# Low parts of fp32 operands subtracted on GpSimd instead of VectorE, in the first two blocks of a gated scan and MLP kernel

## The chip, the core and the metric

The kernel runs on one core of a Trainium2 chip. A core has engines with queues of their own: TensorE (PE: matrix products into PSUM), VectorE (DVE), ScalarE (ACT), GpSimd (POOL) and SyncE (SP), whose queue issues the transfers here. Each engine takes its instructions in the order in which the program gives them, and semaphores make it wait for others. The metric is the device time of one execution in microseconds (us), as a median of several runs. It takes in a little more than the span of the profile, which goes from the first to the last instruction.

## What is computed

A linear attention with a complex gate for each key channel, and on its output an MLP with a piecewise activation:

```
a_n = a * min(|a|, 0.999) / (|a| + 1e-6)          # a complex, (B=4, H=8, S=768, D=48)
for t in range(S):
    S_re, S_im = (ar*S_re - ai*S_im) + outer(k[t], v[t]),  ar*S_im + ai*S_re
    y[t] = q[t] @ S_re
x = y as (3072 tokens, 384)
h = x @ w_in                                       # 384 -> 2048
g = where(h >= 1, h, where(h <= -1, 0, (h + 1)**2 / 4))
out = g @ w_out                                    # 2048 -> 384
```

All data are fp32. The two large products are made from rounded parts: each operand is split into a high part in the format fp32r and a low part, the operand less its high part, and a product is the sum of three matmuls: high by high, low by high and high by low. The change touches how low parts are made.

## The kernel before

**Units and blocks.** The 3072 tokens are 12 units of 256. Two units are a block, so there are six blocks (0 to 5) of T = 512 tokens. For a unit, `gates` makes the decay and the phase of the keys and queries (ScalarE and VectorE), `attend` the scores, masked products and states (TensorE, with `am` and `st` on VectorE), and the result lands transposed in the tile `xr`. For a block, `split` makes xH and xL of `xr`, and `moe` runs the MLP: for each of 16 slices f of the 2048 channels, `gemm1(f)` makes h in PSUM (three matmuls for each of three j; line 1160), the engines make g and its parts gh and gl, and `gemm2(f)` adds their products with the slice of w_out to three sums o in PSUM (line 1235).

**The activation.** In blocks 0 and 1 (`spare`, that is blk < SPARE = 2) ScalarE makes s from h in three instructions (lines 1185, 1195, 1199) and VectorE g = max(h, s) (line 1204). In the other blocks ScalarE has one instruction and VectorE two (1204 and 1212). Then ScalarE copies g to gh in fp32r (1218), and VectorE subtracts: gl = g - gh (1222). h lies in PSUM in two buffers, so gemm1(f + 2) needs g of slice f made; s and g share three buffers, and gh and gl share six.

**The weights.** Sixteen tiles of 128 x 768 (eight of w_in, wi; eight of w_out, wo; each serves two slices f) are loaded once as pairs of 32-bit words and decoded into fp32 by three VectorE instructions in place (`weights`, lines 431, 440, 449). ScalarE copies the high part (455). The low part of the first three tiles (n < LO_PE = 3) is made on TensorE through PSUM; of the 13 others VectorE subtracts it (460). From the fifth tile on, two staging buffers take turns, so the load of a tile waits for the subtraction of the tile two before it.

**The order.** Nothing is issued in the order in which the functions are written. Each `pl.op` notes an instruction for a planner: engine, a price in ns, what it reads and writes. `Plan.order` runs the whole program through a model of the five engines, with the prices and fixed delays between engines (LAT, 200 ns behind POOL); an engine takes of its ready instructions the one that is due first, where due times are worked back from those of the matmuls. The instructions are emitted in the order of the planned starts, so a price that changes can move any instruction of any engine, and what the model does not hold cannot move one. Before the first matmul of block 0, the planner also fills planned gaps of TensorE with small matmuls whose result is not used (line 1290), in numbers that follow from the planned times.

Of the kernel before, what the change touches and what calls it, by code (L numbers as in the profile page):

```python
# [10 lines left out]
F32 = mybir.dt.float32  # L11
# [4 lines left out]
ALU = mybir.AluOpType  # L16
# [274 lines left out]
def dve(n, two=False):  # L291
    return 66 + n / (1.92 if two else 0.96)


def act(n, ptr=False, acc=False, psum=False):
    return (80 if psum else 100) + (92 if ptr else 0) + (92 if acc else 0) + n * (0.77 if psum else 0.84)


def pe32(n):
    return 2 * max(85, n / 1.2 + 5)  # L300


def per(n):
    return n / 2.4 + 16
# [17 lines left out]
def gated_scan_moe(  # L322
    ctx: ExitStack, tc: tile.TileContext, kq, ari, art, v, wl, qn, kn, arn, ain, vn, out
):
    nc = tc.nc
# [38 lines left out]
    def tl(slot, shape, dtype, name, space=None):  # L364
        return pl.tile(
            slot, lambda: (space or sb).tile(shape, dtype, tag=slot, name=name, bufs=1)
        )
# [12 lines left out]
    def turn_of(tag, n):  # L380
        k = seen.get(tag, 0)
        seen[tag] = k + 1
        return f"{tag}{k % n}"

    V_, A_, PE_ = nc.vector, nc.scalar, nc.tensor
# [20 lines left out]
    def load(k, raw, eng="SP"):  # L406
        queue = nc.sync if eng == "SP" else nc.gpsimd
        queue.dma_start(raw.rearrange("p n t -> p (n t)"), wl[k].bitcast(U32))

    def weights(n, kind, i, slot):  # L410
        k = i + (NF // 2 if kind == "o" else 0)
        RAW = tl(slot, [P, 2 * DM, 2], U32, f"raw_{kind}{i}")
        Y = tl("y", [P, 2 * DM], U32, f"y_{kind}{i}")
        W = weight[kind, i] = tl(f"w{kind}{i}", [P, 2, 2, DM], F32R, f"w{kind}_{i}")
        hi, lo = (lambda: W.get()[:, :, 0]), (lambda: W.get()[:, :, 1])
        wide = lambda t: t.rearrange("p (e n) -> p e n", e=2)
        top, low = (lambda: RAW.get()[:, :, 1]), (lambda: RAW.get()[:, :, 0])
        N = 2 * DM
        eng, late = ("SP", 0) if n < 3 else (LOADS, LATE)
        pl.op(  # L420
            eng,
            SOFT_ISSUE if eng == "POOL" else DMA_ISSUE,
            lambda: load(k, RAW.get(), eng),
            w=[RAW],
            dma=P * N * 8 / LOAD,
            late=late,
        )
        pl.op(
            "DVE",
            dve(N, True),  # L430
            lambda: V_.tensor_scalar(
                Y.get(), top(), 3, 0x3FFFFFFF, op0=ALU.logical_shift_left, op1=ALU.bitwise_and
            ),
            r=[RAW],
            w=[Y],
        )
        pl.op(
            "DVE",
            dve(N),
            lambda: V_.scalar_tensor_tensor(  # L440
                low(), low(), 29, Y.get(), op0=ALU.logical_shift_right, op1=ALU.bitwise_or
            ),
            r=[Y],
            w=[(RAW, 0)],
        )
        pl.op(
            "DVE",
            dve(N),
            lambda: V_.scalar_tensor_tensor(
                low(), top(), 0xC0000000, low(), op0=ALU.bitwise_and, op1=ALU.bitwise_or  # L450
            ),
            w=[(RAW, 0)],
        )
        yf = lambda: wide(low().bitcast(F32))
        pl.op("ACT", act(N) + 50, lambda: A_.copy(hi(), yf()), r=[(RAW, 0)], w=[(W, 0)])
        if n >= LO_PE:
            pl.op(
                "DVE",
                dve(N),
                lambda: V_.tensor_tensor(lo(), yf(), hi().bitcast(F32), op=ALU.subtract),  # L460
                r=[(RAW, 0), (W, 0)],
                w=[(W, 1)],
            )
            return
        for e in range(2):
            R = tl("h0", [P, DM], F32, f"rest_{kind}{i}_{e}", ps)

            def rest(e=e, R=R):
                PE_.matmul(R.get(), ident, yf()[:, e], start=True, stop=False)
                PE_.matmul(R.get(), minus, hi()[:, e], start=False, stop=True)  # L470

            i_ = pl.op(
                "PE",
                pe32(DM) + per(DM),
                rest,
                r=[(RAW, 0), (W, 0)],
                w=[R],
                due=FIRST - 30000 + 2000 * n,
            )
            kinds[i_] = "rest"  # L480
            pl.op(
                "ACT",
                act(DM, psum=True),
                lambda e=e, R=R: A_.copy(lo()[:, e], R.get()),
                r=[R],
                w=[(W, 1 + e)],
            )
# [657 lines left out]
    def moe(blk):  # L1145
        XH, XL = split(blk)
        T = len(BLOCKS[blk]) * U
# [5 lines left out]
        def gemm1(f):  # L1153
            H = tl(turn_of("h", 2), [P, T], F32, f"h_{blk}_{f}", ps)
            for j in range(NJ):

                def mms(j=j):
                    sl = slice(j * P, (j + 1) * P)
                    for n, (part, x) in enumerate(((0, XH), (1, XH), (0, XL))):
                        PE_.matmul(  # L1160
                            H.get(),
                            weight["i", f // 2].get()[:, f % 2, part, sl],
                            x.get()[:, j, :],
                            start=j == 0 and n == 0,
                            stop=j == NJ - 1 and n == 2,
                        )

                kinds[len(pl.ops)] = "moe"
                pl.op(
                    "PE",  # L1170
                    3 * per(T),
                    mms,
                    r=[weight["i", f // 2]] + [(x, (ub, j)) for x in (XH, XL) for ub in range(len(BLOCKS[blk]))],
                    w=[H],
                    due=t0 + STEP * (f + j / 6),
                )
            SS = tl(turn_of("s", 3), [P, T], F32, f"s_{blk}_{f}")
            G = tl(turn_of("s", 3), [P, T], F32, f"g_{blk}_{f}")
            GH = tl(turn_of("gg", 6), [P, T], F32R, f"gh_{blk}_{f}")
            GL = tl(turn_of("gg", 6), [P, T], F32R, f"gl_{blk}_{f}")  # L1180
            spare = blk < SPARE
            pl.op(
                "ACT",
                act(T, ptr=True, psum=True),
                lambda: A_.activation(  # L1185
                    SS.get(), H.get(), AF.Relu, bias=c_half, scale=-0.5 if spare else 0.5
                ),
                r=[H],
                w=[SS],
            )  # L1190
            if spare:
                pl.op(
                    "ACT",
                    act(T, ptr=True),
                    lambda: A_.activation(SS.get(), SS.get(), AF.Relu, bias=c_one, scale=-1.0),
                    w=[SS],
                )
                pl.op(
                    "ACT", act(T), lambda: A_.activation(SS.get(), SS.get(), AF.Square), w=[SS]
                )  # L1200
            pl.op(
                "DVE",
                dve(T),
                lambda: V_.tensor_tensor(G.get(), H.get(), SS.get(), op=ALU.max),  # L1204
                r=[H, SS],
                w=[G],
            )
            if not spare:
                pl.op(
                    "DVE",  # L1210
                    dve(T),
                    lambda: V_.scalar_tensor_tensor(  # L1212
                        G.get(), SS.get(), 1.0, G.get(), op0=ALU.min, op1=ALU.mult
                    ),
                    r=[SS],
                    w=[G],
                )
            pl.op("ACT", act(T), lambda: A_.copy(GH.get(), G.get()), r=[G], w=[GH])  # L1218
            pl.op(
                "DVE",  # L1220
                dve(T),
                lambda: V_.tensor_tensor(GL.get(), G.get(), GH.get().bitcast(F32), op=ALU.subtract),  # L1222
                r=[G, GH],
                w=[GL],
            )
            gs[f] = (GH, GL)
# [25 lines left out]
        for k in range(NF + LAG):  # L1252
            if k < NF:
                gemm1(k)
            if k >= LAG:
                gemm2(k - LAG)
# [52 lines left out]
    for n, (kind, i) in enumerate(todo):  # L1309
        weights(n, kind, i, ("xH1", "xL1", "xH0", "xL0")[n % 4] if n < HOME else ("xH1", "xL1")[n % 2])  # L1310
# [269 lines left out]
```

## Time and profile before

| | |
|---|---|
| Runs shown: median (lowest to highest) of 3 | 578.95 us (577.08 to 580.69) |
| Profiled execution: span | 575.6 us; the page gives no time of its own beside the span |
| Mean granted TensorE clock | 0.998 of full |
| First matmul of block 0 (L1160) | starts at 70.4 us |
| gl subtractions on VectorE (L1222) | 96, of 687 ns, 66.0 us in all; 32 of them belong to blocks 0 and 1 |
| Low parts of weights on VectorE (L460) | 7 of wo, 951 ns, and 6 of wi, 944 ns; 12.3 us in all, from 42.7 to 153.8 us |
| Transfers | 77.42 MB, mean 134 GB/s |

Durations of VectorE instructions in the profile overlap a little: one of 512 columns is shown with 0.69 us, but the next begins 0.60 us after it; one of 768 columns with 0.95 us, the next after 0.87. Matmuls overlap far more: one of 512 columns is shown with 0.39 us, and nine of them take 2.04 us. In the chain of waits the pieces don't overlap. A line such as L460 is a line of the kernel, and a tile is named without its buffer's number (`wo<-raw_o,wo` reads the staging buffer and the high part and writes the low part). In the windows view a row has the stretch, its length, then busy us and count for each engine, the granted clock, the share of the transfer engines and GB/s; asked for one line of the kernel, it has only the engines that run this line.

### The profile page before, as it was taken

The page shows a single profiled execution, that of the slowest core. Times are in us where ns is not written, and L with a number is a line of the kernel's source. Part 1 is how long each engine was busy: PE and PEld are TensorE (multiplying, and loading weights), DVE is VectorE, ACT ScalarE, POOL GpSimd, SP SyncE. Part 2 cuts the span into 40 slices and gives each one's busy share as a digit, 9 for nine tenths or more (in the row PEclk, how much of TensorE's full clock was granted, in tenths as well). Part 3 has the DMA queues.
Part 4 walks back from the last instruction along what each step waited for, and adds up shares of the span by engine and source line. Part 5 has one row for each costly group of instructions (what it writes and reads, how often), then busy time and mean ns, then how long its engine had stood idle before and what let it go on. Part 6 is the DMA issues. An engine that isn't in the chain of part 4 may idle for free.

```text
span 575.6 us, 9984 instructions
## 1 busy us (share of the span) xinstructions
PE 561.4 (98%) x3922; PEld 478.4 (83%) x3922; DVE 434.5 (75%) x625; ACT 406.1 (71%) x654; POOL 1.7 (0%) x20
## 2 busy tenths in 40 slices
PE   8999999999999999999999999999999999999995
PEld 7798978888888888888888888888888888888883
DVE  4999999999979498579589878887885544455452
ACT  7776799887998998975576666667643333369972
POOL 1000000000000000000000000000000000000000
PEclk9999999999999999999999999999999999999999
DMA  8676571773641614712601613402312200078811
GB/s 352 250 198 192 163 262 55 192 282 114 188 173 48 195 68 125 237 57 82 174 2 52 202 56 102 153 2 85 114 56 72 74 1 7 21 265 309 298 42 61
DMA packets 23527, 77.42 MB, mean 134 GB/s; under 512 B 4528, under 2 KB 10288, under 8 KB 23472
## 3 DMA queue, kind: packets, MB, share of 16 engines
q1 hardware_dynamic: 23472, 76.70, 40.8%
q8 instruction: 33, 0.54, 0.4%
q14 instruction: 22, 0.18, 0.1%
HBM read 51.90 MB, written 4.72 MB: 98 GB/s over the span
## 4 chain that ended last, share of the span: by engine, by line
PE 78%; DVE 12%; ACT 5%; DMA 2%; issue 1%; SPq 0%; ACTq 0%; DVEq 0%
PE o L1235 30%; PE h L1160 29%; PE sc L989 6%; PE yp L1038 3%; PE yp L1030 3%; PE dp L962 2%; PE tp L933 1%; PE idle L1290 1%; ACT ai L608 1%; DVE kq L725 1%; DMA xr<-xr 1%; DMA ai<-in_art_dram 1%; DVE g L1204 1%; ACT x L608 1%; DVE raw_i L440 1%
## 5 line engine op out<-in xcount | busy, mean ns | idle before, releaser
L1160 PE MATMUL h<-xH,wi 128*128 128x512 f32 x576 | 180.6, 395 | 1.2 <-DVE g L1204 0.9
L1235 PE MATMUL o<-gh,wo 128*128 128x512 f32 x576 | 180.4, 394 | 0.0
L1160 PEld LDWEIGHTS h<-xH,wi 128*128 128x128 f32 x576 | 106.2, 188 | 22.6 <-DVE g L1204 1.1
L1235 PEld LDWEIGHTS o<-gh,wo 128*128 128x128 f32 x576 | 106.3, 188 | 21.6 <-issue 0.7
L1204 DVE TENSOR_TENSOR g<-h,s 128x512 f32<-128x512 f32 x96 | 65.9, 687 | 63.1 <-ACT s L1185 45.6
L1160 PE MATMUL h<-xL,wi 128*128 128x512 f32 x288 | 112.6, 391 | 0.0
L1235 PE MATMUL o<-gl,wo 128*128 128x512 f32 x288 | 112.5, 391 | 0.0
L1185 ACT ACTIVATE s<-h,cst 128x512 f32<-128x512 f32 x96 | 65.7, 685 | 42.0 <-PE h L1160 38.9
L1218 ACT CAST gh<-g 128x512 fp32r<-128x512 f32 x96 | 59.1, 616 | 46.0 <-DVE g L1212 43.6
L1222 DVE TENSOR_TENSOR gl<-g,gh 128x512 fp32r<-128x512 f32 x96 | 66.0, 687 | 31.9 <-ACT gh L1218 31.8
L1160 PEld LDWEIGHTS h<-xL,wi 128*128 128x128 f32 x288 | 54.1, 188 | 12.1 <-DVE xL L1137 0.4
L1235 PEld LDWEIGHTS o<-gl,wo 128*128 128x128 f32 x288 | 54.1, 188 | 11.6
L608 ACT ACTIVATE ai<-ai 128x768 f32<-128x768 f32 x49 | 41.2, 843 | 19.1 <-DVE ai L777 8.6
L989 PE MATMUL sc<-hd 96*128 96x128 f32 x384 | 49.6, 278 | 0.0
L989 PEld LDWEIGHTS sc<-hd 96*128 96x128 f32 x384 | 47.0, 192 | 2.2
L1212 DVE SCALAR_TENSOR_TENSOR g<-s,g 128x512 f32<-128x512 f32 x64 | 44.2, 691 | 1.8
L1038 PE MATMUL yp<-am,V 128*64 128x128 f32 x384 | 35.5, 273 | 0.2 <-DVE am L997 0.2
L997 DVE TENSOR_TENSOR am<-sc,sums 128x512 f32<-128x512 f32 x48 | 32.5, 683 | 3.1 <-PE sc L989 2.8
L1290 PE MATMUL idle<-sums,ident 128*128 128x128 f32 x238 | 31.3, 291 | 1.7 <-POOL sums masks.py:66 1.7
L1030 PE MATMUL yp<-hd,st 96*64 96x128 f32 x320 | 32.1, 278 | 0.3 <-DVE am L997 0.3
L1290 PEld LDWEIGHTS idle<-sums,ident 128*128 128x128 f32 x238 | 30.3, 206 | 2.5 <-POOL sums masks.py:66 1.7
L402 ACT ACT_TABLE_LOAD x21 | 26.9, 1283 | 0.4
(104 smaller groups left out, 651.6 us busy)
## 6 DMA issues: line engine op xcount, KB each, us to landing
chk<-in_wl_dram SPq DMA_DIRECT2D x16, 768.0 KB, 5.2
kq<-in_kq_dram SPq DMA_DIRECT2D x12, 768.0 KB, 4.7
ai<-in_ari_dram SPq DMA_DIRECT2D x10, 768.0 KB, 6.1
hd<-x SPq DMA_DIRECT2D x24, 288.0 KB, 4.1
hd<-kq SPq DMA_DIRECT2D x24, 288.0 KB, 4.9
raw_i<-in_wl_dram SPq DMA_DIRECT2D x8, 768.0 KB, 4.6
raw_o<-in_wl_dram SPq DMA_DIRECT2D x8, 768.0 KB, 5.8
V<-in_v_dram SPq DMA_DIRECT2D x12, 384.0 KB, 3.2
```

Of the source, the lines that this page charges most:

```text
L608: lambda: A_.activation(out(), src(), f, **kw),
L989: PE_.matmul(SC.get()[:, i, :], t[:, 0, cs], t[:, 1, cs], start=True, stop=True)
L1030: PE_.matmul(o_, st.get().rearrange("p h e -> p (h e)")[:, lo : lo + 64], head(h)[:, 1, cs], start=True, stop=False,)
L1038: PE_.matmul(o_, V.get()[:, c, lo : lo + 64], ams[pr // 2].get()[:, 2 * (pr % 2) + e, :], start=st is None, stop=True,)
L1160: PE_.matmul(H.get(), weight["i", f // 2].get()[:, f % 2, part, sl], x.get()[:, j, :], start=j == 0 and n == 0, stop=j == NJ - 1 and n == 2,)
L1185: lambda: A_.activation(SS.get(), H.get(), AF.Relu, bias=c_half, scale=-0.5 if spare else 0.5),
L1204: lambda: V_.tensor_tensor(G.get(), H.get(), SS.get(), op=ALU.max),
L1212: lambda: V_.scalar_tensor_tensor(G.get(), SS.get(), 1.0, G.get(), op0=ALU.min, op1=ALU.mult),
L1218: pl.op("ACT", act(T), lambda: A_.copy(GH.get(), G.get()), r=[G], w=[GH])
L1222: lambda: V_.tensor_tensor(GL.get(), G.get(), GH.get().bitcast(F32), op=ALU.subtract),
L1235: PE_.matmul(PO[m].get(), weight["o", f // 2].get()[:, f % 2, part, sl], g.get(), start=f == 0 and n == 0, stop=f == NF - 1 and n == 2,)
L1290: PE_.matmul(idle["h1"], ident, mask, start=True, stop=True)
```

## The change

Two subtractions go from VectorE's queue to GpSimd's, with their operands, results and dependences as they were: the low part of the 13 weight tiles with n >= 3, and gl of the 32 slices of blocks 0 and 1. In blocks 2 to 5 gl stays on VectorE. The planner gets a price for the moved instructions: 250 + 2.2 n ns for n columns, in place of 66 + n/0.96.

```diff
+def pool(n):
+    return 250 + 2.2 * n
+
...
         if n >= LO_PE:
             pl.op(
-                "DVE",
-                dve(N),
-                lambda: V_.tensor_tensor(lo(), yf(), hi().bitcast(F32), op=ALU.subtract),
+                "POOL",
+                pool(N),
+                lambda: nc.gpsimd.tensor_tensor(
+                    lo(), yf(), hi().bitcast(F32), op=ALU.subtract
+                ),
                 r=[(RAW, 0), (W, 0)],
                 w=[(W, 1)],
             )
...
             pl.op(
-                "DVE",
-                dve(T),
-                lambda: V_.tensor_tensor(GL.get(), G.get(), GH.get().bitcast(F32), op=ALU.subtract),
+                "POOL" if spare else "DVE",
+                pool(T) if spare else dve(T),
+                lambda: (nc.gpsimd if spare else V_).tensor_tensor(
+                    GL.get(), G.get(), GH.get().bitcast(F32), op=ALU.subtract
+                ),
                 r=[G, GH],
                 w=[GL],
             )
```

## The prediction

> **What bounds the kernel now.** I read the page first: busy shares and slices. Busy is a share of the span, and a slice is 14.4 us.
>
> ```profile
> PE 561.4 (98%) x3922; PEld 478.4 (83%) x3922; DVE 434.5 (75%) x625; ACT 406.1 (71%) x654; POOL 1.7 (0%) x20
> PE   8999999999999999999999999999999999999995
> DVE  4999999999979498579589878887885544455452
> POOL 1000000000000000000000000000000000000000
> ```
>
> TensorE (PE) is covered from end to end, VectorE (DVE) is full only in slices 2 to 11, that is until about 160 us, and GpSimd (POOL) does nothing after its constants. So whatever the change brings has to come out of the first 160 us. A busy PE need not be an effective one, so I went on to the chain of waits in the first 150 us (start, length, what):
>
> ```profile
> 49.72 0.66 PE tp L933 x8
> 50.38 1.81 PE sc L989 x16
> ...
> 83.07 1.75 DVE kq L725
> ...
> 106.38 0.60 DVE gl L1222
> ...
> 141.28 0.86 DVE wi L460
> 142.14 0.61 DVE am L997
> ...
> 144.55 0.22 PE yp L1038 x4
> 144.77 0.92 PE dp L962 x32
> 145.69 2.28 PE o L1235 x9
> 147.98 2.04 PE h L1160 x9
> ```
>
> From 83 to 142 us the chain is mostly a queue of VectorE instructions, and the two that the change moves (L1222 and L460) are links of it, at 0.60 and 0.86 us each. From 143 us on it is all TensorE. That looks as if each microsecond taken from VectorE were a microsecond of the end. To test that, I counted what TensorE has to do in 80 to 150 us. The windows view gives first all engines, then the instructions of L1160, L1235, L989, L1038, L1030, L962 and L933 alone (PE's count is the first number in brackets):
>
> ```profile
> 80.00:150.00 70.00, 69.69 (x553) 59.30 (x553) 69.11 (x96) 62.02 (x97) 0.00 (x0) 1.00 0.55 181
> 80.00:150.00 70.00, 27.39 (x108) 20.00 (x108) 1.00 0.55 181
> 80.00:150.00 70.00, 27.69 (x109) 19.80 (x109) 1.00 0.55 181
> 80.00:150.00 70.00, 6.38 (x48) 5.97 (x48) 1.00 0.55 181
> 80.00:150.00 70.00, 6.24 (x64) 4.05 (x64) 1.00 0.55 181
> 80.00:150.00 70.00, 6.43 (x64) 3.82 (x64) 1.00 0.55 181
> 80.00:150.00 70.00, 4.35 (x128) 4.27 (x128) 1.00 0.55 181
> 80.00:150.00 70.00, 3.30 (x32) 3.08 (x32) 1.00 0.55 181
> ```
>
> The chain's rows give the pace at which TensorE takes each kind: 2.04/9 = 0.227 us for a matmul of the two large products, 1.81/16 = 0.113 for a score, 0.22/4 = 0.055 for a value, 0.92/32 = 0.029 for a key product, 0.66/8 = 0.083 for a transpose. So 217 x 0.227 + 48 x 0.113 + 128 x 0.055 + 128 x 0.029 + 32 x 0.083 = 49.3 + 5.4 + 7.0 + 3.7 + 2.7 = 68.1 us of 70. Both engines are full here: TensorE stands still for 1.9 us in this stretch, at full granted clock. VectorE's work could shrink by a lot and TensorE would return no more than that; if VectorE's work grows, nothing covers it. This lopsidedness decides more than the size of the saving.
>
> **The change, part by part.** The next rows are the windows view again: 20 to 160 us for VectorE and all others, then for L460, L1222, L1204 and L997 alone; then L460 in 20 to 70 us; then all engines in 160 to 250 us.
>
> ```profile
> 20.00:160.00 140.00, 136.12 (x1169) 118.59 (x1168) 137.16 (x190) 117.49 (x181) 0.00 (x0) 1.00 0.57 184
> 20.00:160.00 140.00, 12.32 (x13) 1.00 0.57 184
> 20.00:160.00 140.00, 10.92 (x16) 1.00 0.57 184
> 20.00:160.00 140.00, 10.93 (x16) 1.00 0.57 184
> 20.00:160.00 140.00, 10.98 (x17) 1.00 0.57 184
> 20.00:70.00 50.00, 2.84 (x3) 1.00 0.59 179
> 160.00:250.00 90.00, 90.00 (x588) 75.86 (x587) 65.62 (x94) 83.59 (x137) 0.00 (x0) 1.00 0.43 133
> ```
>
> Removed from VectorE until 160 us: all 13 weight subtractions and the 16 of block 0. At the chain's pace that is 13 x 0.86 + 16 x 0.60 = 11.2 + 9.6 = 20.8 us. The 16 of block 1 fall after 160 us, where VectorE is busy for 65.6 us of 90 and TensorE for all 90: their removal is worth nothing, and cover of 24 us stands behind it.
>
> Added: the same 29 (later 16) subtractions on POOL, whose queue is otherwise empty, so nothing stands behind a waiting POOL instruction but the next subtraction. No DMA issue is added or moved; no queue is passed. A weight's staging buffer is released by POOL and not by VectorE, about a microsecond later, and its next load waits that long in SP's queue with the loads behind it; the 13 subtractions are spread over 110 us, more than 8 us apart, so I cost this at nothing (without that cover, 1 us for each).
>
> What POOL needs for 512 and 768 columns of two operands no row of before shows. The nearest rows are its fills and its masks:
>
> ```profile
> L341 POOL MEMSET cst<- 128x1 f32 x8 | 0.3, 98 | 0.0
> masks.py:66 POOL TENSOR_SCALAR_AFFINE_SELECT sums<-sums 128x128 f32<-128x128 f32 x1 | 0.3, 293 | 0.0
> ```
>
> The start costs 98 ns, and (293 - 98)/128 = 1.5 ns goes with each column of one operand. Two operands take between that and the double, 3.0. The new pool() in the diff prices 250 + 2.2 n ns, in between, and I take that as POOL's length: 1.38 and 1.94 us, so 16 x 1.38 + 13 x 1.94 = 47 us of 140. POOL keeps up easily.
>
> [...]
>
> The unknown that matters is whether POOL holds VectorE up while it reads. In before the two never work at once after 10 us, so bound it from both sides. Low end: not at all, and VectorE is relieved of 20.8 us. High end: VectorE stands still whenever a POOL subtraction reads and the VectorE instruction due reads only SBUF. Of the VectorE time that stays, 137.2 - 12.3 - 10.9 = 114 us, at least L1204 and L997 (10.9 + 11.0) take an operand from PSUM; the other 80% does not. With the start left out, POOL reads 16 x 512 + 13 x 768 = 18,176 columns: 27 us at 1.5 ns, 40 us at 2.2, 55 us at 3.0. Four fifths of that is 22, 32 and 44 us, against 20.8 us relieved. The ledger of VectorE thus runs from -20.8 to +23 us, and at the two likelier paces it is +1 and +11. A VectorE instruction that reads two operands passes 0.60/512 = 1.2 ns a column, so if the two had to take turns at reading, each would cost the other about the time that it reads. I take +5, between the two likelier values and nearer to the lower one, because smaller PSUM readers than the two rows quoted are not counted.
>
> **What of it reaches the end.** VectorE's +5 falls into stretches where TensorE has next to no slack, so I put 4 us of it on the end, after the wait of TensorE that disappears beside it:
>
> ```profile
> 77.64 0.73 PE L1160 MATMUL h<-xH,wi 128*128 128x512 f32 x2 [0.93 <-DVE g L1204]
> ...
> 78.97 0.68 DVE L1222 TENSOR_TENSOR gl<-g,gh 128x512 fp32r<-128x512 f32 x1
> ...
> 79.81 0.62 PE L1235 MATMUL o<-gh,wo 128*128 128x512 f32 x2
> ```
>
> The 0.93 us is a wait for g behind other VectorE work, of the kind that relief removes. The other two rows show a new risk: the product with wo starts 0.2 us after gl is there. With POOL gl comes 1.38 - 0.60 = 0.8 us later, plus its own wait for a VectorE instruction in progress. The planner knows the 0.8 us and can put 2.04 us of the next h product in between, so I cost it at nothing; without that cover it is a lag of 1 to 2 us, once, since a TensorE that has fallen behind finds the later gl ready.
>
> The sum: span 575.6 + 4 = 579.6 us. The median of the runs shown is 578.95, that is 3.35 us over the span, which the change does not touch; so 583 us.
>
> **The rivals.** First, VectorE is not held up at all. For it speaks that POOL and VectorE are separate engines with separate queues, against it nothing in this trace. Its ledger is then -20.8 us, but TensorE can return only what it loses: 1.9 us in 80 to 150, the 0.93 us above, and in 20 to 70 us at most the three L460 (3 x 0.86 = 2.6) that may stand ahead of an attention step. That is -5.4 us at best and about -3 likely: 576 us, from 573.5 to 578. This is the rival with the other sign, and it decides where VectorE loses clearly less than 20.8 us / 18,176 columns = 1.1 ns for each column that POOL reads.
>
> Second, POOL stops VectorE for its whole length, starts included: 47 x 0.8 = 38 us against 20.8, a ledger of +17, of which 10 to 12 reach the end, since VectorE's own gaps and the work that is not urgent take the rest. That is 590 us, from 586 to 594. For it speaks that 80% of what is left on VectorE reads SBUF alone; against it, that start and end of an instruction need not read. [...]
>
> Third, the late gl: TensorE lags by 1 to 2 us behind POOL while VectorE breaks even, 580.5 us. That the change does nothing, because the planner gives the 20.8 us to other VectorE work, is the first rival with a gain of zero, 579.
>
> **How the numbers follow.** Forecast, partly held up: 0.36, with 579 to 587 as its own range. Wholly held up: 0.31. Not held up: 0.26. Late gl: 0.07. A measurement of this kernel tells about 1% (5.8 us) from no change. Slower by more than that, above 584.7, are nearly all of the wholly held case and a fifth of the forecast: 0.30 + 0.08 = 0.38. Faster, below 573.2, takes more than TensorE has to return, so only four in ten of the not held case, through another order at the start: 0.10. The rest, 0.52, is within 1%. The range 573.5 to 592 leaves out those and the upper end of the wholly held case, just under 0.2.
>
> **What would show it.** L460 and L1222 of the first two blocks on POOL, 45 of them, at 1.4 and 1.9 us. Right, if VectorE's SBUF-only instructions (L440, L449, L834) become longer or stand further apart beside POOL, while L1204 and L997 keep 0.68 us; and if VectorE in 20 to 160 us is about as full as before with 29 instructions fewer. The first large product then starts at about its old time, and the loss collects between 80 and 160 us. Wrong towards faster, if those lengths stay and VectorE shows gaps in slices 2 to 11. Wrong towards slower, if lengths grow by more than POOL reads, or TensorE shows waits for POOL at L1235 beyond 2 us in all.

## The result, and the profile after

The changed kernel takes 601.09 us (median of four runs, 600.52 to 601.72) against 579.31 us for the kernel before on the same chip (577.08 to 580.69). The ratio is 1.0385, with a 95% interval of 1.0359 to 1.041. It is slower, which the prediction gave a chance of 0.38, and by 21.8 us where 4 were forecast; that is above its range, which ended at 592. The profiled span is 599.0 us, 23.4 more than before.

First the page of the changed kernel: busy time by engine, and the slices (15.0 us each now) with the clock granted to TensorE.

```profile
PE 570.2 (95%) x3916; PEld 481.5 (80%) x3916; DVE 436.6 (73%) x580; ACT 407.2 (68%) x654; POOL 78.9 (13%) x65
PE   8988989898899999989999999999999999999995
DVE  4999999779966749738868978798787464544552
POOL 1013032654531422220000000000000000000000
PEclk9998999898999999999999999999999999999999
```

VectorE (DVE) has 45 instructions fewer, 580 for 625, and yet 436.6 us of busy time for 434.5: some of the others became longer. TensorE (PE) shows eights in slices 2 to 11, where before it had only nines. And its clock, which before stood at full speed (0.998 on the mean), has dips (0.990). The windows view shows the same stretches as before the prediction (all engines: PE, PEld, DVE, ACT, POOL, then the clock):

```profile
20.00:160.00 140.00, 124.63 (x1023) 107.52 (x1022) 129.13 (x145) 101.86 (x152) 44.35 (x23) 0.96 0.51 163
80.00:150.00 70.00, 62.78 (x451) 52.87 (x450) 61.88 (x67) 55.78 (x86) 30.61 (x17) 0.95 0.46 154
160.00:250.00 90.00, 88.73 (x623) 73.69 (x624) 63.58 (x77) 80.24 (x129) 27.73 (x18) 1.00 0.36 108
```

In 80 to 150 us TensorE was busy for 69.69 us before and is for 62.78 now. VectorE did not become the full engine in its place: it went from 69.11 to 61.88. Both stand idle in part: TensorE waits for VectorE's am and g and for POOL's gl, and VectorE in front of g for s (5.1 us in this stretch), which ScalarE makes from TensorE's h. Next VectorE's groups in 20 to 180 us, apart by shape:

```profile
L1003 DVE TENSOR_TENSOR am<-sc,sums 128x512 f32<-128x512 f32 x18 | 12.1, 680 | 0.5 <-PE sc L995 0.5
L1210 DVE TENSOR_TENSOR g<-h,s 128x512 f32<-128x512 f32 x16 | 10.9, 681 | 6.4 <-ACT s L1205 6.4
L453 DVE SCALAR_TENSOR_TENSOR raw_o<-raw_o 128x768 uint32<-128x768 uint32 x8 | 10.3, 1282 | 0.1
L762 DVE TENSOR_TENSOR_SCAN ai<-ai,state,cst 128x256 f32<-128x256 f32 x9 | 9.8, 1129 | 0.5 <-ACT ai L614 0.5
...
L435 DVE TENSOR_SCALAR y_o<-raw_o 128x768 uint32<-128x768 uint32 x8 | 8.3, 1036 | 1.4 <-DMA raw_o<-in_wl_dram 1.4
```

and the same instructions of the kernel before, in 20 to 160 us (the line numbers after are 4 to 8 higher):

```profile
L997 DVE TENSOR_TENSOR am<-sc,sums 128x512 f32<-128x512 f32 x17 | 11.4, 679 | 0.0
L1204 DVE TENSOR_TENSOR g<-h,s 128x512 f32<-128x512 f32 x16 | 10.9, 683 | 0.5 <-ACT s L1199 0.4
...
L449 DVE SCALAR_TENSOR_TENSOR raw_o<-raw_o 128x768 uint32<-128x768 uint32 x8 | 7.6, 952 | 0.1
...
L756 DVE TENSOR_TENSOR_SCAN ai<-ai,state,cst 128x256 f32<-128x256 f32 x9 | 6.3, 736 | 0.0
...
L431 DVE TENSOR_SCALAR y_o<-raw_o 128x768 uint32<-128x768 uint32 x8 | 4.4, 549 | 0.0
```

The two that take an operand from PSUM, am and g, keep 0.68 us. Among those that read SBUF alone some are longer: the decode of a weight 1282 ns on the mean for 952, the scan 1129 for 736, the first decode step 1036 for 549. The lengthening of all VectorE instructions that start before 280 us, each against the mean before of the same operation, tiles and shape, is 31.3 us; some 25 us of that lies before 180 us. It sits in 31 instructions that are longer by more than 0.1 us, and each of the 31 began while a POOL subtraction was under way. 46 VectorE instructions began so; of the other 15, which kept their lengths, 13 are am, g or st, which read PSUM, and two began in the last 0.2 us of POOL's instruction. A mean hides what it looks like for one. The timeline of the changed kernel (start, length, then in brackets the idle time before and who ended it):

```profile
42.10 2.16 POOL L464 TENSOR_TENSOR wi<-raw_i,wi 128x768 fp32r<-128x768 f32 x1 [39.87 <-ACT wi L459]
...
42.48 2.60 DVE L453 SCALAR_TENSOR_TENSOR raw_o<-raw_o 128x768 uint32<-128x768 uint32 x1
...
45.01 0.55 DVE L435 TENSOR_SCALAR y_i<-raw_i 128x768 uint32<-128x768 uint32 x1
...
45.47 0.68 DVE L1003 TENSOR_TENSOR am<-sc,sums 128x512 f32<-128x512 f32 x1
...
46.21 0.55 PE L939 MATMUL tp<-ident,hd 96*128 96x96 f32 x4 [2.95 <-DVE am L1003]
```

The VectorE instruction of 0.95 us starts while POOL works and lasts until 45.08, that is, 0.82 us past POOL's end at 42.10 + 2.16 = 44.26: it stood until POOL's instruction had ended and then did its work. One decode step later comes am, which TensorE has been waiting for: 2.95 us of standing, where the same wait took 0.82 us before:

```profile
42.66 0.95 DVE L460 TENSOR_TENSOR wi<-raw_i,wi 128x768 fp32r<-128x768 f32 x1
...
43.53 0.68 DVE L997 TENSOR_TENSOR am<-sc,sums 128x512 f32<-128x512 f32 x1
...
44.27 0.55 PE L933 MATMUL tp<-ident,hd 96*128 96x96 f32 x4 [0.82 <-DVE am L997]
```

Of the 2.13 us by which this wait grew, 2.60 - 0.95 = 1.65 are the hold. The rest is about the 0.46 us of the decode step L435, which the new order put ahead of am. What that wait does to the clock is seen if TensorE's time is laid out in stretches of 3.41 us, the length that the three falls to half clock before 160 us have in this trace (the windows view; PE busy is the first number after the length, the clock the third from the end):

```profile
44.05:47.46 3.41, 1.25 (x10) 1.06 (x10) 3.41 (x5) 1.75 (x3) 1.59 (x2) 1.00 0.87 198
108.97:112.38 3.41, 0.89 (x9) 0.65 (x11) 3.38 (x3) 2.21 (x4) 2.47 (x2) 1.00 0.49 164
139.69:143.10 3.41, 1.25 (x17) 0.83 (x17) 3.41 (x5) 1.96 (x5) 1.00 (x2) 1.00 0.03 11
156.75:160.17 3.42, 1.85 (x9) 1.16 (x7) 3.28 (x4) 0.47 (x2) 1.37 (x1) 1.00 0.93 341
47.46:50.87 3.41, 3.20 (x44) 3.20 (x46) 3.38 (x6) 0.80 (x2) 1.27 (x1) 0.51 0.36 88
112.38:115.79 3.41, 3.41 (x44) 3.41 (x42) 1.87 (x3) 3.41 (x7) 1.53 (x2) 0.50 0.41 129
143.10:146.51 3.41, 3.41 (x50) 3.41 (x48) 3.41 (x3) 3.34 (x5) 1.80 (x1) 0.50 0.15 28
```

Behind each of the three stretches in which TensorE was busy for only 0.89 to 1.25 us of 3.41, the next 3.41 us run at half clock: 3 x 3.41/2 = 5.1 us of TensorE's work lost. (The first of these half-clock rows begins 0.07 us early, hence its 0.51.) Behind one with 1.85 busy the clock stayed. The waits in the three are the 2.95 us for am above, 2.73 us of the product with wo for POOL's gl, and 2.15 us of the values yp for am.

The loss builds up from the first such wait on. Taking the moment at which ScalarE copies g of a slice, the changed kernel is late by 5.1, 8.5, 12.1 and 15.6 us at slices 0, 4, 8 and 12 of block 0, by 20.0 and 21.4 at slices 0 and 4 of block 1, and by 23 to 25 from slice 8 on to the end.

### The profile page after: what moved, and what is told of

Same layout as the page of the kernel before. It is cut to its first block, busy times and chain, and to the rows that moved or that the text cites. A ratio compares the mean times of both kernels' runs of the same rounds, so it can differ in the third digit from the quotient of the medians.

```text
span 599.0 us, 10054 instructions
## 1 busy us (share of the span) xinstructions
PE 570.2 (95%) x3916; PEld 481.5 (80%) x3916; DVE 436.6 (73%) x580; ACT 407.2 (68%) x654; POOL 78.9 (13%) x65
## 4 chain that ended last, share of the span: by engine, by line
PE 64%; DVE 5%; DMA 4%; ACT 3%; issue 1%; POOL 0%; SPq 0%; DVEq 0%; ACTq 0%
PE o L1243 26%; PE h L1166 25%; PE sc L995 5%; PE yp L1036 2%; PE yp L1044 2%; DMA hd<-x 2%; PE dp L968 2%; PE tp L939 1%; DMA out_dram<-ob 1%; DVE ai L762 1%; ACT ai L614 1%; DMA hd<-kq 1%; DVE g L1210 1%; DVE y_o L435 1%; DVE raw_o L453 0%
## 5 line engine op out<-in xcount | busy, mean ns | idle before, releaser
L1243 PEld LDWEIGHTS o<-gh,wo 128*128 128x128 f32 x576 | 106.1, 188 | 21.4 <-issue 0.7
L1228 DVE TENSOR_TENSOR gl<-g,gh 128x512 fp32r<-128x512 f32 x64 | 44.1, 688 | 25.9 <-ACT gh L1224 25.8
L1228 POOL TENSOR_TENSOR gl<-g,gh 128x512 fp32r<-128x512 f32 x32 | 47.3, 1478 | 103.7 <-ACT gh L1224 80.8
L1044 PE MATMUL yp<-am,V 128*64 128x128 f32 x384 | 38.0, 288 | 0.2 <-DVE am L1003 0.2
L1036 PE MATMUL yp<-hd,st 96*64 96x128 f32 x320 | 33.4, 287 | 4.2 <-DVE am L1003 4.1
L1298 PEld LDWEIGHTS idle<-sums,ident 128*128 128x128 f32 x232 | 29.4, 205 | 2.5 <-POOL sums masks.py:66 1.7
```

The costliest lines, as they stand in the source:

```text
L1036: PE_.matmul(o_, st.get().rearrange("p h e -> p (h e)")[:, lo : lo + 64], head(h)[:, 1, cs], start=True, stop=False,)
L1044: PE_.matmul(o_, V.get()[:, c, lo : lo + 64], ams[pr // 2].get()[:, 2 * (pr % 2) + e, :], start=st is None, stop=True,)
L1228: lambda: (nc.gpsimd if spare else V_).tensor_tensor(GL.get(), G.get(), GH.get().bitcast(F32), op=ALU.subtract),
L1243: PE_.matmul(PO[m].get(), weight["o", f // 2].get()[:, f % 2, part, sl], g.get(), start=f == 0 and n == 0, stop=f == NF - 1 and n == 2,)
L1298: PE_.matmul(idle["h1"], ident, mask, start=True, stop=True)
```

## The experiments

The theories: **A**, POOL's reads hold VectorE up, and the holds hit what TensorE waits for. **B**, the planner's new order is what costs. **C**, gl comes late to TensorE. **L**, VectorE's ledger decides, work taken off less holds put on. Where an edit is to the kernel before, its line numbers are those of before.

**Order and engine apart.** The new order, but the subtractions issued on VectorE at POOL's places in it:

```diff
-                lambda: nc.gpsimd.tensor_tensor(
+                lambda: V_.tensor_tensor(
...
-                lambda: (nc.gpsimd if spare else V_).tensor_tensor(
+                lambda: V_.tensor_tensor(
```

> The planner sees the changed kernel (subtractions on POOL at its prices), so the order on every queue is that of the changed kernel, but the 45 subtractions are issued on VectorE. POOL reads nothing, so nothing can hold VectorE up. Theory A (POOL's reads hold VectorE up, and that alone makes the loss of 22 us): VectorE has its old work again and no hold, so 578 to 586 us. Theory B (the order is the fault: it was planned for a VectorE that is 20.8 us lighter, and VectorE never is): the order is the same, so 595 to 603 us.

The old order, and the subtractions issued on POOL:

```diff
-                "POOL",
-                pool(N),
+                "DVE",
+                dve(N),
...
-                "POOL" if spare else "DVE",
-                pool(T) if spare else dve(T),
+                "DVE",
+                dve(T),
```

> The planner sees the kernel before (subtractions on VectorE at its prices), so the order on every queue is that of before, but the 45 subtractions are issued on POOL. Theory A: the hold is as in the changed kernel (some 25 to 30 us of lengthened VectorE instructions against 20.8 us of relief), so 590 to 603 us. Theory B: the plan keeps a place of 0.60 or 0.87 us on VectorE for each subtraction, which about pays for the hold, so 579 to 586 us.

Measured: 597.88 us for the first (ratio 1.0299, 1.0238 to 1.0359), 594.71 for the second (1.026, 1.0225 to 1.0296); before 579.36. Each alone costs most of the loss, 18.5 and 15.4 us; both theories got their number, and neither explains the other's. The first has no POOL work, and no VectorE instruction is longer than before; its windows:

```profile
20.00:70.00 50.00, 45.95 (x400) 42.16 (x400) 42.65 (x59) 30.78 (x42) 0.00 (x0) 0.83 0.50 155
70.00:160.00 90.00, 83.52 (x651) 70.41 (x651) 83.82 (x113) 73.44 (x112) 0.00 (x0) 0.98 0.50 169
```

In 20 to 70 us the clock is at 0.83 (one wait of 2.16 us for am, then 17 us at half speed): 0.17 x 50 = 8.5 us, and slice 0 of block 0 is late by 8.6. So an order that was planned for a VectorE without these 20.8 us loses about as much when VectorE has them as the changed kernel loses. In the second the lengthening is 29.4 us in 29 instructions: the holds come with the POOL instructions, in either order.

**A planner that knows of the hold.** Of POOL's price, 55% was noted as an empty VectorE instruction ahead of it, so that the order leaves room:

```diff
+            held = pl.op("DVE", HELD * pool(N), lambda: None, r=[(RAW, 0), (W, 0)])
...
-                pool(N),
+                (1 - HELD) * pool(N),
...
+                after=[held],
```

> As the changed kernel, on POOL, but the planner is told of the hold: for each subtraction it keeps 55% of POOL's price free on VectorE (0.76 and 1.07 us), and POOL has the other 45%; nothing is issued for that place. Theory B: a plan that knows the loss gives it back almost wholly, 579 to 587 us. Theory A: a better plan cannot take the hold away, 592 to 603 us.

Measured: 596.94 us (1.0298, 1.0265 to 1.0331; before 579.36), with 32.1 us of lengthening. That is a loss of 17.6 us for the changed kernel's 21.8: room in the plan gave back 4 us at most, and the holds stayed. Whether they struck beside the room that was left for them is not shown.

**One half at a time.** Of the changed kernel first the weights' part is undone, then instead gl's; last the weights' part, and gl stays on POOL in block 1 alone:

```diff
-                "POOL",
-                pool(N),
-                lambda: nc.gpsimd.tensor_tensor(
+                "DVE",
+                dve(N),
+                lambda: V_.tensor_tensor(
```

```diff
-                "POOL" if spare else "DVE",
-                pool(T) if spare else dve(T),
-                lambda: (nc.gpsimd if spare else V_).tensor_tensor(
+                "DVE",
+                dve(T),
+                lambda: V_.tensor_tensor(
```

```diff
-                "POOL" if spare else "DVE",
-                pool(T) if spare else dve(T),
-                lambda: (nc.gpsimd if spare else V_).tensor_tensor(
+                "POOL" if blk == 1 else "DVE",
+                pool(T) if blk == 1 else dve(T),
+                lambda: (nc.gpsimd if blk == 1 else V_).tensor_tensor(
```

> Of the change only gl of blocks 0 and 1 is on POOL, planned so; the 13 weight tiles stay on VectorE. If the loss goes with the time that POOL reads beside a full VectorE (theory A): gl of block 0 is 16 x 1.3 = 21 us of the 45 us of POOL work before 160 us, so a bit under half of the 22 us, 586 to 592 us. If it comes from gl reaching TensorE later (theory C): nearly the whole loss, 596 to 602 us. If gl costs nothing and the weights are at fault: 577 to 582 us.

> Of the change only the 13 weight subtractions are on POOL, planned so; gl of all blocks stays on VectorE. If the two halves add up to the changed kernel's 22 us (gl alone cost 12.6): 587 to 591 us. If the loss of the whole is one thing that either half already causes (a plan upset by any change): 592 to 600 us.

> Only gl of block 1 is on POOL, planned so; weights and block 0 stay on VectorE. In block 1 VectorE is idle for 24 us of 90 in the kernel before. If such idle time covers the holds: 578 to 581 us. If holds cost also there, as the lag that the changed kernel gathers in block 1 suggests (3 us): 581.5 to 584 us.

Measured: 591.96 us (1.021, 1.0178 to 1.0243), 592.03 (1.0236, 1.0201 to 1.0272; before 579.32) and 581.19 (1.0041, 1.0019 to 1.0063; before 579.03), with 18.4, 15.6 and 5.3 us of lengthening (before 579.36 for the first). The halves cost 12.6 and 12.7 us, 25 together for 21.8 in one. So the weights alone take a little longer than the 587 to 591 us that were expected if the halves add up, and lie at the lower edge of the other range; these times do not decide between the two. The weights alone give no late gl, so C is at most a part. Behind 160 us, where VectorE has gaps, 16 subtractions on POOL cost 2.2 us, a time between the two ranges that were named.

**Relief alone.** The low parts are not made on any engine, in the old order; the matmuls read the high parts in their place, so TensorE's work is the same:

```diff
-                lambda: V_.tensor_tensor(lo(), yf(), hi().bitcast(F32), op=ALU.subtract),
+                lambda: None,
...
-                lambda: V_.tensor_tensor(GL.get(), G.get(), GH.get().bitcast(F32), op=ALU.subtract),
+                lambda: spare or V_.tensor_tensor(GL.get(), G.get(), GH.get().bitcast(F32), op=ALU.subtract),
...
-                            weight["o", f // 2].get()[:, f % 2, part, sl],
-                            g.get(),
+                            weight["o", f // 2].get()[:, f % 2, part * full("o", f), sl],
+                            (GH if blk < SPARE else g).get(),
```

> The order of the kernel before, and the 45 subtractions are left out altogether: for these tiles the low part is not made, and the matmuls that would read it read the high part instead, so that TensorE's work stays the same and what is computed lacks these low parts. VectorE is relieved of 20.8 us before 160 us, and nothing holds it up. Theory A (relief is worth little because TensorE is full, holds cost where they strike, and the two do not net out): 573.5 to 578 us. Theory L (VectorE's ledger is what counts): the relief comes back to a large part, below 570 us.

(full is true for the three tiles n < 3, and the matmul with w_in has the same edit.) The same in the new order, with the planner's entries for POOL left in:

```diff
-                lambda: nc.gpsimd.tensor_tensor(
-                    lo(), yf(), hi().bitcast(F32), op=ALU.subtract
-                ),
+                lambda: None,
```

> The order of after (planned with the 45 subtractions on GpSimd), but they are made on no engine: the low parts of the 13 weight tiles and of g in blocks 0 and 1 are not made, and the matmuls that read them read the high parts instead, so that TensorE has the same number of matmuls. VectorE is now as light as the planner took it for. Theory X (the order is sound; it costs 18.5 us with the subtractions on VectorE, and 21.8 with them on GpSimd, because VectorE then carries 20 to 30 us that the plan does not hold): 573 to 578, like the same relief in the order of before (575.85). Theory Y (the new order is bad in itself, whatever VectorE carries): 584 or more. Between them: both take part. A re-plan that turns the relief into time would show less than 573.

Measured: 575.85 us (0.9942, 0.9923 to 0.9961; before 579.32) and 577.36 us (0.9981, 0.9962 to 0.9999; before 578.97). That is the most that a move of these 45 instructions can bring in these two orders: 3.5 us in the old one and 1.6 in the new. The second also settles what the run with the new order on VectorE had left open. Its windows view,

```profile
20.00:70.00 50.00, 46.93 (x512) 42.95 (x511) 47.55 (x64) 37.19 (x53) 0.00 (x0) 1.00 0.62 192
70.00:160.00 90.00, 89.25 (x657) 76.00 (x658) 71.57 (x100) 83.01 (x132) 0.00 (x0) 1.00 0.56 180
```

has the new order with TensorE busy for 89.25 us of 90 at full clock. The order is sound for the VectorE that it was planned for; it costs 18.5 us when VectorE carries what the plan took off it.

**Holds alone.** The kernel before, VectorE's subtractions in place, and 45 subtractions of no use on POOL behind them (high part less itself, into a buffer that is not read again until it is refilled; the code is shortened):

```diff
+                    nc.gpsimd.tensor_tensor(wide(top().bitcast(F32)), hi().bitcast(F32), hi().bitcast(F32), op=ALU.subtract),
...
+                    and nc.gpsimd.tensor_tensor(G.get(), GH.get().bitcast(F32), GH.get().bitcast(F32), op=ALU.subtract),
```

> The order and the work of the kernel before, with all subtractions on VectorE, and beside each of the 45 a subtraction of the same size on POOL whose result nobody reads (it reads the high part twice and writes into a tile that is no longer needed). So the hold without the relief. Theory A: about the same loss as with the old order and the subtractions on POOL (e2: 15 us) and a little more, since relief is worth 1 to 5 us: 595 to 602 us. Theory L (the ledger counts): 15 + 20.8 us more than before, 610 to 618 us. If POOL's reads are harmless: 579 to 582 us.

Measured: 604.04 us (1.0439, 1.0407 to 1.0471; before 579.32), 2 us above the range of theory A and 6 below that of L. With 25.6 us of lengthening the kernel is 24.7 us slower: 0.96 us of the end for each us of hold. POOL also keeps the staging and g buffers longer here; the next run, which keeps them in the same way, tells how much that can be worth. The timeline has the same figure as after the change, in an order that was not touched:

```profile
42.54 1.78 POOL L462 TENSOR_TENSOR raw_i<-wi 128x768 f32<-128x768 f32 x1 [40.30 <-PE sc L997]
...
42.91 2.22 DVE L461 TENSOR_TENSOR wi<-raw_i,wi 128x768 fp32r<-128x768 f32 x1
...
45.79 0.55 PE L941 MATMUL tp<-ident,hd 96*128 96x96 f32 x4 [2.10 <-DVE am L1005]
```

**Reads or POOL work of any kind.** The same, with two fills in place of each subtraction, so that POOL writes but reads nothing:

```diff
+                    [nc.gpsimd.memset(top().bitcast(F32), 0.0) for _ in range(2)],
...
+                    and [nc.gpsimd.memset(G.get(), 0.0) for _ in range(2)],
```

> As e7 (order and work of the kernel before, and 45 additional pieces of work on POOL that nobody needs), but each piece is two fills of the same tile in place of a subtraction: POOL writes and reads nothing. By the fills of the profile (98 ns and 0.84 ns a column) a piece takes about 1.1 or 1.5 us. If only POOL's reads hold VectorE up: instructions with two operands in SBUF (the scans, L440, L449, L725, L834) keep their lengths, only those that VectorE runs at two columns a cycle (L431, L626, L771: 0.55 us for 768) may be held, 580 to 587 us. If POOL's writes hold it up as well: nearly e7's loss in proportion to the time, 592 to 600 us.

Measured: 581.83 us (1.0058, 1.004 to 1.0076; before 579.03), and no lengthening (-0.1 us over all). The windows view and VectorE's groups in 20 to 160 us:

```profile
20.00:160.00 140.00, 134.95 (x1161) 117.20 (x1159) 134.84 (x185) 115.04 (x175) 38.67 (x54) 1.00 0.57 178
```

```profile
L449 DVE SCALAR_TENSOR_TENSOR raw_o<-raw_o 128x768 uint32<-128x768 uint32 x8 | 7.6, 952 | 0.1
...
L759 DVE TENSOR_TENSOR_SCAN ai<-ai,state,cst 128x256 f32<-128x256 f32 x9 | 6.3, 736 | 0.0
```

POOL is busy for 38.67 us, nearly as long as with the useless subtractions (42.69 in the same stretch), and 952 and 736 ns are the lengths of before. The TENSOR_SCALAR of 768 columns, named as those that may be held, keep 550 ns too. So in these two runs the holds go with POOL's reading: 25.6 us of lengthening beside subtractions, none beside fills. The 2.8 us that remain were not followed up; buffers that come free later can be in them, and at that size explain little of the 24.7.

**Shorter holds.** The kernel before, with the 45 subtractions issued on POOL in the old order, each cut into pieces of 128 columns (gl is shown, shortened; a weight tile is cut in the same way):

```diff
-                lambda: V_.tensor_tensor(GL.get(), G.get(), GH.get().bitcast(F32), op=ALU.subtract),
+                lambda k=128 if spare else T: [
+                    (nc.gpsimd if spare else V_).tensor_tensor(GL.get()[:, c : c + k], ...)
+                    for c in range(0, T, k)
+                ],
```

> As e2 (order of the kernel before, subtractions on POOL), but each in pieces of 128 columns: six for a weight tile, four for gl. By e2's trace a piece takes 0.17 + 128 x 2.2 ns = 0.45 us, so POOL works some 40% longer in all, but no single hold is longer than about 0.5 us. If the loss comes from long holds that strike an urgent instruction: less than e2's 15 us, 582 to 589 us. If the sum of the held time counts, however it is cut: 594 to 602 us.

Measured: 596.46 us (1.0315, 1.029 to 1.034; before 579.03). The number expected if the sum of held time counts came out, but for another reason. The lengthening fell from 29.4 to 11.5 us, so short holds do help VectorE. What took their place is seen in POOL's groups and in the list of waits (total, times, longest):

```profile
L1236 POOL TENSOR_TENSOR gl<-g,gh 128x128 fp32r<-128x128 f32 x128 | 86.4, 707 | 60.2 <-ACT gh L1231 45.0 <-issue 15.1
```

```profile
PE o L1256 <- POOL gl L1236: 6.6, 6, 2.8
```

A gl in four pieces takes 4 x 0.71 = 2.8 us, and TensorE waits for it six times, 6.6 us in all. This is theory C, which the whole subtractions of the changed kernel showed only twice. The rest of the 17.4 us was not divided up.

**The order of before as a lucky one.** The planner's price of gl in blocks 0 and 1 raised by 5%, and nothing moved:

```diff
-                dve(T),
+                1.05 * dve(T) if spare else dve(T),
```

> The kernel before with nothing moved; only the planner's price for gl in blocks 0 and 1 is 5% higher on VectorE (30 ns each), which reorders some instructions. Theory B2 (the order of before is a lucky one and any other costs several us): 584 to 595 us. Otherwise: 577 to 582 us.

Measured: 578.42 us (0.9991, 0.9964 to 1.0019; before 579.32). So another order need not cost anything, and the order of before is not a lucky one in that sense.

## Why the prediction was wrong

**The bound: right.** "VectorE's work could shrink by a lot and TensorE would return no more": taking the 45 instructions off everything returned 3.5 us in the old order; the rival of a VectorE that is not held up had put "-5.4 us at best and about -3 likely".

**POOL's lengths: right.** 1.38 and 1.94 us were taken; the short ones of the trace, those that were not held themselves, take about 1.29 and 1.85 us, so (1.85 - 1.29)/256 = 2.2 ns a column, the price of pool(). The means are longer, because POOL is held by VectorE as well: the subtraction of a weight in the timeline above began at 42.10, while a VectorE instruction of 0.95 us, begun at 41.61, was under way, and it took 2.16 us for 1.85.

```profile
L1228 POOL TENSOR_TENSOR gl<-g,gh 128x512 fp32r<-128x512 f32 x32 | 47.3, 1478 | 103.7 <-ACT gh L1224 80.8 <-PE sc L995 10.9 <-PE o L1243 4.1
L464 POOL TENSOR_TENSOR wo<-raw_o,wo 128x768 fp32r<-128x768 f32 x7 | 16.5, 2350 | 30.1 <-ACT wo L459 30.1
```

**VectorE's ledger: right in size, in part by luck.** "I take +5": some 25 us of lengthening before 180 us, less 20.8 us relieved, is about +4. As a mechanism, though, the rival "POOL stops VectorE for its whole length" was nearer than the forecast's partial hold: the VectorE instruction at 42.48 us stands until POOL has finished, 2.60 us for 0.95, while beside the fills, which read nothing, this decode step keeps its mean of 952 ns. The ledger stayed small because only 46 VectorE instructions began beside POOL and 31 of them were caught, and no term of the prediction stands for that. Nor would that rival have given the time: its 586 to 594 us end below 601.09.

**The step that failed: "VectorE's +5 falls into stretches where TensorE has next to no slack, so I put 4 us of it on the end".** It nets the relief and the holds as if a microsecond of the one were worth a microsecond of the other. Measured apart in the old order they are worth -3.5 and +24.7 us, and the prediction's own reading said why: TensorE has 1.9 us to return, and nothing covers work that is added. A microsecond taken off VectorE alone was worth 3.5/20.8 = 0.17 us, a microsecond of hold 24.7/25.6 = 0.96. Beside holds the relief is worth more: from the run with holds alone (604.04) to the old order with the subtractions on POOL (594.71) VectorE loses the same 45 subtractions, and 9.3 us come back, though the holds are then 3.8 us longer (29.4 for 25.6). At 0.96 that makes 9.3 + 3.6 = 12.9 us of the 20.8, an estimate across two runs. So the relief is worth little alone and more beside holds, but it was not worth its full size anywhere, as the forecast has it.

**What the prediction did not see.** First, a hold (1.0 us on the mean of the 31, 1.68 us the longest) strikes single instructions, and where am or g stands behind them in VectorE's queue, TensorE stands with it, as at 42 us. Averages over 140 us do not show that. Second, behind three waits of 2.15 to 2.95 us the clock stood at half, 5.1 us in all; the prediction costed waits at their length alone. Third, the price change gave a new order that had already spent the relief: with VectorE as light as planned it runs in 577.36 us, with VectorE's 20.8 us put back in 597.88. The changed kernel's VectorE carries 31.3 us of holds which the plan does not know of, and loses 21.8. With the re-plan the loss is thus 21.8 - 15.4 = 6.4 us greater than with about as much hold (29.4 us) in the old order.

**The small terms.** The late gl was costed at nothing, with 1 to 2 us if its cover went: TensorE waited for POOL's gl twice, 2.9 us in all, and one of these waits, of 2.73 us, is among the three behind which the clock fell to half. It came when gl of a slice stood in POOL's queue behind a weight:

```profile
106.83 2.67 POOL L464 TENSOR_TENSOR wo<-raw_o,wo 128x768 fp32r<-128x768 f32 x1 [5.41 <-ACT wo L459]
...
109.47 1.97 POOL L1228 TENSOR_TENSOR gl<-g,gh 128x512 fp32r<-128x512 f32 x1
...
111.49 0.49 PE L1243 MATMUL o<-gl,wo 128*128 128x512 f32 x1 [2.73 <-POOL gl L1228]
```

"Nothing stands behind a waiting POOL instruction but the next subtraction" was true, and the next subtraction was the urgent one. Of the signs that were named, the longer SBUF readers and the unchanged am and g showed; a VectorE as full as before did not (129.13 us for 137.16, with 6.4 us in front of g), and the first large product started at 74.06 us, not at 70.41. A sign of "wrong towards slower" came too: the waits for POOL at the product with wo are beyond 2 us in all (2.9).

Three readings were loose. Block 1 was put at nothing, with a cover of 24 us; on POOL its 16 subtractions cost 2.2 us. The 13 weight subtractions are not "more than 8 us apart": in the kernel before they begin 6.0 to 17.2 us apart, and the first two after the change 4.0. The term that rested on this, a staging buffer that comes free later, was put at nothing: VectorE waits once for the load of a weight, 1.4 us, but the new order without any subtraction has 3.2 us of such waits, so this is not shown to come from POOL. And the 3.35 us between median and span belong to different executions: in the runs shown the time is about 2 us over the span of the same execution. The forecast of 583 does not hang on it, since it is the median of before plus 4.

**What stays open.** No run takes the half clock away and leaves the waits, so how the 21.8 us divide between standing, half clock and what follows from both is read from the trace, not shown. In the profiled execution of the new order on VectorE the half clock before 70 us alone is 8.5 us, nearly half of its 18.5. No version was found that is clear of noise and faster than the kernel before with all low parts made: in the two orders tried the most to be had from these instructions is 3.5 us, by not having them at all.

## What to carry to other kernels

Cost what is taken from an engine and what is put on it apart, each against the slack of the engine that sets the end; here a microsecond of the one did not cancel a microsecond of the other. Before work goes from VectorE to GpSimd, look at whether both would read SBUF at the same time; here a hold lasted until the GpSimd instruction had ended (2.60 us for 0.95), and a planner that was not told of it had already given the saving away. Run the change with the moved work left out: that run bounds the gain in its order, and here it would have ended the matter at 0.6%.

## What the hardware showed that was not expected

The clock dropped on waits of 2.15 to 2.95 us, shorter than the 3.41 us for which it then stayed down. It fell at 47.53, 112.38 and 143.10 us, each time for 3.41 us (and at 597.1, behind the last matmul); 64.85 us are 19 times 3.413 and 30.72 us 9 times, so the three falls lie on one grid of that length. A stretch of this grid in which TensorE was busy for 1.25 us of 3.41 was enough, one with 1.85 was not, and from 30 us on and up to the last 10 all others have 2.14 or more, with the clock full behind them. The kernel before has one fall, at 573.5 us, behind its last matmul; on a grid laid from there it has 2.49 or more in every stretch from 30 us on and up to the last 10. In the new order on VectorE the fall at 46.2 us follows a stretch with about 1.2. What decides between 1.25 and 1.85 us is not shown by these three. How long the clock stays down is open: in the changed kernel it came back after one stretch, in the new order on VectorE after five (17.07 us), though TensorE was busy throughout in the last four of them.

A fill on GpSimd, which did not hold VectorE, was held by it in places. In the run with fills two of 512 columns take 1.11 us, but 1.48 where VectorE has a TENSOR_SCALAR of 768 columns with one operand (0.55 us) between them:

```profile
79.75 1.48 POOL L1228 MEMSET g<- 128x512 f32 x2 [4.06 <-DVE gl L1226]
...
80.22 0.55 DVE L431 TENSOR_SCALAR y_i<-raw_i 128x768 uint32<-128x768 uint32 x1
...
83.12 1.75 DVE L728 TENSOR_TENSOR kq<-kq,x 128x1536 f32<-128x1536 f32 x1
83.26 1.11 POOL L1228 MEMSET g<- 128x512 f32 x2 [2.03 <-DVE gl L1226]
```

Beside the two-input product at 83.12 us the fills keep their length.
